# Heads of output groups 0 and 1 back to back, one root for all second-half statistics, and a new order of all queues, in a fused attention and gated-MLP kernel

## The chip, the cores and the metric

The kernel runs on one NeuronCore of one Trainium2 chip. The metric is the device time of one execution in microseconds (us), lower is better.

The engines in the profile: PE is the tensor engine's matmuls, PEld its weight loads, DVE the vector engine, ACT the scalar engine, POOL the GpSimd engine, SP the engine that issues most DMAs. A "q" behind a name means that engine's instruction sequencer.

## The reference

```python
x = A_x                                     # (1, 2048, 512), bf16
xn = layernorm(x)
# A: 32 heads of width 16; each position attends to 8 positions, 2 apart, itself included
q, k, v = split(xn @ wqkv)
attn = softmax(q.k[pos - 2*w] / 4, over w = 0..7)
A = concat(sum_w attn * v[pos - 2*w]) @ wo
# B: a gated MLP whose gate mixes over positions
z  = gelu(xn @ w_in)                        # 2048 x 1376
z1 = z[:, :688];  z2 = layernorm(z[:, 688:])
B = (z1 * (w_sp @ z2 + b_sp)) @ w_out       # w_sp is 2048 x 2048
out = x + A + B
```

## The kernel before

The kernel is written as small steps, each of which emits the instructions of one piece of work, and as one long string, `ORDER`, that lists the steps. Each engine gets its instructions in the order of that string, and in the traces each engine's work stands in that order, so the string is the plan of five queues at once. The 2048 positions are 16 tiles of 128 rows; four tiles form an output group.

The steps that matter here:

| step | engine | what it does |
|---|---|---|
| `z`, `X` | PE | one tile of `xn @ w_in` (second half, first half), 8 matmuls of 344 columns |
| `zg`, `zs` | ACT | gelu of a `z` tile with its sum; its squares with their sum |
| `nw`, `st` | DVE (`st.3`, `st.4`: ACT) | mean, variance and inverse root of the 16 tiles' statistics |
| `N` | DVE | normalise one tile of z2 |
| `p`, `a`, `b` | DVE | products q*k and their sums over the head width |
| `L`, `Lc` | PE, ACT | logits: matmuls in 32-column tiles, then a copy out |
| `V`, `Vc` | PE, ACT | values: matmuls in 32-column tiles, then a copy out |
| `G`, `Gi`, `U`, `T` | PE, ACT, DVE, DMA | gate: 32 matmuls of one tile; plus bias; times z1; transposed by DMA |
| `A` | DVE | 60 products and sums of attention with v, 15 for each group |
| `O`, `Or`, `Oh` | PE | output of a group: heads (64 matmuls in 32-row tiles), remainder (8 matmuls, 24 rows), two halves of 10 full matmuls |
| `Fe`, `F`, `s` | ACT, DVE, DMA | copy a group's output out of PSUM, add x, store |

The program divides eight banks of PSUM, the memory that the matmuls write to: three buffers of two banks (the large pool) and two of one (the small pool).

```python
ps_mm  = ctx.enter_context(tc.tile_pool(name="ps_mm",  bufs=3, space=PSUM))   # 2 banks each
ps_aux = ctx.enter_context(tc.tile_pool(name="ps_aux", bufs=2, space=PSUM))   # 1 bank each
```

The statistics of z2: the twelve tiles of blocks 0 to 2 got their root on the vector engine by Newton's method, the last four on the scalar engine by logarithm and exponential.

```python
def z2_newton(j0, j1):
    b = slice(4 * j0, 4 * j1 + 4)
    y, h, a = zrstd[:, b], zvar[:, b], zm2[:, b]
    turn = [lambda: V.tensor_tensor(a, y, y, ALU.mult),
            lambda: V.scalar_tensor_tensor(a, a, -0.5, h, ALU.mult, ALU.mult),
            lambda: V.scalar_tensor_tensor(y, a, 1.5, y, ALU.add, ALU.mult)]
    return [lambda: V.tensor_scalar(h, h, EPS, None, ALU.add),
            lambda: V.tensor_scalar(y.bitcast(I32), h.bitcast(I32), -0.5, float(0x5f3759df), ALU.mult, ALU.add),
            *turn, *turn, *turn]

def z2_log():                                  # z2_exp follows: exp(-0.5 * log)
    b = slice(12, 16)
    need_table("exp")                          # loads another ACT table where needed
    A.activation(zm2[:, b], zvar[:, b], ACT.Ln, bias=eps_t[:])
```

The heads of a group take two buffers of the large pool; the last group takes one of the large pool, both of the small one, and a cut more.

```python
def out_heads(o):
    last = o == 3
    pos = []
    for tb in range(TB):                                   # TB = 4
        if last and tb >= 2:
            pa = ps_aux.tile([P, TBS], F32, name="pa", tag="aux")
            pos.append(pa[:])
            if tb == 3:
                pb = ps_mm.tile([P, 2, TBS], F32, name="pb", tag="mm")
            continue
        if tb % 2 == 0:
            pmm = ps_mm.tile([P, 2, TBS], F32, name="po", tag="mm")
        pos.append(pmm[:, tb % 2, :])
    # ... (cuts of the last group left out)
    for d in (*range(8, DH), *range(8)):
        for tb in range(TB):
            for pc, cs in cuts[tb]:
                PE.matmul(pc, op[32 * tb:32 * tb + 32, d, o * P:(o + 1) * P],
                          wo_r[32 * tb:32 * tb + 32, d, cs],
                          start=(d == 8), stop=False, tile_position=(32 * tb, 0))
```

Parts of `ORDER`: the logits 5, 6 and 7, the heads of groups 0 and 1, and the end (each ... is a cut):

```
... S0.4 U1 L5 L6 R0 X6 Lc5 ...
... A2 wo1.3 T2 A3 L7 Gi5 ...
... w14 A17 X11 Gi7 T6 A18 O0 Xg11 A19 w10 A20 A21 Or0 Oh0.0 U7 A22 A23 X15 Fe0.0 Fe0.1 F0.0 Oh0.1 A24 s0.0 ...
... A32 s0.1 w15 A33 A34 s0.3 w12 A35 O1 Gi14 A36 T9 U11 A37 xr1 U10 Or1 A38 X14 T8 A39 Oh1.0 ...
... O3 Fe2.2 Fe2.3 F2.2 F2.3 F2.0 s2.3 s2.2 s2.1 s2.0 Or3 Oh3.0 Oh3.1 F3.0 F3.1 s3.0 s3.1 end
```

`end` adds and stores the last three pieces (two from SP, one from ACT).

## Time and profile before

Three runs of the kernel before had a median of 202.78 us (202.71 to 203.77). The span in the table runs from the first to the last instruction of the profiled execution and is about 1.7 us shorter than that execution's time (201.6 against 203.31 us).

| of the profile before | |
|---|---|
| span | 201.6 us |
| PE busy | 197.2 us, 98% |
| DVE busy | 185.4 us, 92% |
| ACT busy | 106.9 us, 53% |
| first z tile starts | 22.66 us |
| last matmul starts | 198.54 us |
| ACT table loads | 10 |

The page's engine line (busy us, share of the span, instructions), and its first line of the chain that ended last:

```profile
PE 197.2 (98%) x1667; PEld 124.9 (62%) x1667; DVE 185.4 (92%) x261; ACT 106.9 (53%) x174; POOL 4.1 (2%) x14
...
PE 93%; DMA 2%; DVE 2%; issue 0%; ACTq 0%
```

A high PE share alone proves little. The Trainium skill ("Perfetto Trace Analysis", "Tensor Engine Instruction (MATMUL, LD_WEIGHTS)") says that a matmul's end in a trace is estimated, not observed, and the same page ("Identifying the Most-Contended Engine") advises against matmul busy time as a measure. The trace agrees: a matmul of 344 columns is recorded as 0.31 us long, and the next one starts after 0.146 us. So I read starts. The next fence is the timeline of PE before, four cuts of it; the columns are start, duration, engine, line, operation, what it writes and reads, shape, and how many instructions were merged:

```profile
108.55 0.40 PE L365 MATMUL pl<-r_pr,rsel 128*32 128x512 bf16 x4
108.88 2.51 PE L240 MATMUL pz<-w_z,xnT 128*128 128x344 bf16 x16
111.23 9.50 PE L454 MATMUL pg<-z,r_qk 128*128 128x344 bf16 x64
120.56 1.33 PE L240 MATMUL pz<-w_z,xnT 128*128 128x344 bf16 x8
121.73 9.50 PE L454 MATMUL pg<-z,r_qk 128*128 128x344 bf16 x64
131.06 1.33 PE L240 MATMUL pz<-w_z,xnT 128*128 128x344 bf16 x8
132.32 3.63 PE L507 MATMUL po<-r_lg,r_pr 32*128 32x512 bf16 x64
135.79 0.60 PE L516 MATMUL po<-r_w,r_uz 24*128 24x512 bf16 x8
136.32 2.33 PE L537 MATMUL po<-r_w,r_uz 128*128 128x512 bf16 x10
...
155.91 3.63 PE L507 MATMUL po<-r_lg,r_pr 32*128 32x512 bf16 x64
...
190.25 0.39 PE L507 MATMUL po<-r_lg,r_pr 32*128 32x512 bf16 x2
...
198.15 0.64 PE L537 MATMUL pb<-r_w,r_uz 128*128 128x224 bf16 x5
```

Compare starts. Eight matmuls of 344 columns take 1.17 us (120.56 to 121.73), but 1.26 us when heads follow (131.06 to 132.32). The 0.09 us more is the way into 32-row mode. The four logits at 108.55 take 0.33 us (0.332 in the single records) where a group of four takes 0.216: the 0.12 us more is the way out. There is no other gap: PE is full from 8.7 us to the end, save for these small steps. I call one way in and out an excursion. Before has eight.

The single records of the weight loads show one thing that differs at such a step. Inside a mode the load for the next matmul starts beside the matmul before it, 144 ns ahead of its own matmul. Before the first heads matmul at 132.32 and before the first full one behind them (136.32) it starts only 4 ns ahead, and so (2 to 5 ns) at every other change of mode in the traces of before.

The vector engine is nearly as full. It waits at 102 us for a gate tile (the bracket gives the idle time before, and what ended it):

```profile
101.93 0.49 DVE L468 TENSOR_TENSOR r_uz<-gs,r_uz 128x640 bf16<-128x640 bf16 x1 [1.62 <-ACT gs L460]
...
186.81 2.55 DVE L433 TENSOR_TENSOR r_pr<-r_pr 128x2048 bf16<-128x2048 bf16 x2
```

The second of these lines ends with the last heads sum, at 189.36 us (186.81 + 2.55). The heads of group 3, which need it, start at 190.25 (in the fence of PE). The slack is 0.9 us.

### The profile page before, as it was taken

The numbers are of one execution on the slowest core, as the hardware profiler recorded it, in microseconds if no ns is written. First come the engines' busy times: TensorE is split into PE (matmuls) and PEld (weight loads), VectorE is DVE, ScalarE is ACT, GpSimd is POOL, SyncE is SP. The second block draws the span as 40 slices with busy tenths as digits, with TensorE's granted clock in tenths as the row PEclk, the third lists the DMA queues.
The fourth block names the chain that finished last, engine by engine and source line by source line (L and its number), as shares of the span: only waits on it lengthen the run. The fifth ranks groups of instructions, "written<-read, shape, count | busy, mean of one in ns | idle before, by whom it ended". The sixth has DMA issues, their size and how long they took to land.

```text
span 201.6 us, 4043 instructions
## 1 busy us (share of the span) xinstructions
PE 197.2 (98%) x1667; PEld 124.9 (62%) x1667; DVE 185.4 (92%) x261; ACT 106.9 (53%) x174; POOL 4.1 (2%) x14
## 2 busy tenths in 40 slices
PE   7899999999999999999999999999999999999994
PEld 2689856656656666666656666644666446664562
DVE  5799699999999999999979999999999999999815
ACT  3575999989999886080383285134712152121400
POOL 3000000400000000000000000000000000000000
PEclk9999999999999999999999999999999999999999
DMA  4994447000794000659949808991243998059363
GB/s 129 340 298 77 90 94 249 0 0 0 134 209 79 0 3 0 125 176 222 205 101 263 166 3 202 195 204 25 75 106 78 234 182 119 0 144 194 77 207 133
DMA packets 66306, 25.91 MB, mean 129 GB/s; under 512 B 56240, under 2 KB 66032, under 8 KB 66032
## 3 DMA queue, kind: packets, MB, share of 16 engines
q1 hardware_dynamic: 65568, 25.19, 55.3%
q10 hardware_dynamic: 720, 0.47, 0.7%
q8 instruction: 13, 0.21, 0.5%
q14 instruction: 5, 0.04, 0.1%
HBM read 10.13 MB, written 2.10 MB: 61 GB/s over the span
## 4 chain that ended last, share of the span: by engine, by line
PE 93%; DMA 2%; DVE 2%; issue 0%; ACTq 0%
PE pg L454 37%; PE pz L240 19%; PE pq L311 13%; PE po L537 8%; PE pv L415 7%; PE po L507 6%; DMA r_x<-in_A_x_dram 2%; PE pl L365 1%; DVE r_pr L525 1%; PE po L516 1%; PE pb L507 1%; DVE stats L211 1%; PE pt L226 1%; ACTq L168 0%; PE pa L311 0%
## 5 line engine op out<-in xcount | busy, mean ns | idle before, releaser
L454 PE MATMUL pg<-z,r_qk 128*128 128x344 bf16 x448 | 66.6, 309 | 0.0
L454 PEld LDWEIGHTS <-r_qk 128*128 128x128 bf16 x448 | 43.8, 98 | 21.8
L240 PE MATMUL pz<-w_z,xnT 128*128 128x344 bf16 x256 | 40.0, 309 | 0.0
L460 ACT ACTIVATE gs<-pg,b_col 128x688 bf16<-128x688 f32 x16 | 13.2, 834 | 48.2 <-PE pg L454 48.2
L429 DVE TENSOR_TENSOR r_pr<-r_x,r_w 128x2048 bf16<-128x2048 bf16 x32 | 38.4, 1219 | 0.3
L433 DVE TENSOR_TENSOR r_pr<-r_pr 128x2048 bf16<-128x2048 bf16 x28 | 34.0, 1218 | 0.4
L240 PEld LDWEIGHTS <-xnT 128*128 128x128 bf16 x256 | 24.6, 98 | 14.4 <-issue 1.9
L311 PE MATMUL pq<-xnT,r_w 128*128 128x256 bf16 (+1 forms) x176 | 29.1, 317 | 0.1
L345 DVE TENSOR_TENSOR r_pr<-r_qk 128x2048 bf16<-128x2048 bf16 x24 | 28.2, 1218 | 0.3 <-ACT r_qk L321 0.3
L311 PEld LDWEIGHTS <-r_w 128*128 128x128 bf16 x184 | 20.2, 114 | 7.4 <-DMA r_w<-in_A_wqkv_dram 0.6
L321 ACT CAST r_qk<-pq 128x1024 bf16<-128x1024 f32 (+1 forms) x16 | 15.4, 990 | 1.9 <-PE pq L311 1.9
L537 PE MATMUL po<-r_w,r_uz 128*128 128x512 bf16 x70 | 16.0, 379 | 0.0
L302 ACT ACTIVATE r_uz<-pz 128x688 bf16<-128x688 f32 x16 | 11.7, 742 | 7.3 <-PE pz L240 7.2
L507 PE MATMUL po<-r_lg,r_pr 32*128 32x512 bf16 x224 | 14.5, 375 | 0.0
L520 ACT CAST r_qk<-po 128x512 bf16<-128x512 f32 x12 | 6.4, 589 | 14.7 <-PE po L537 14.6
L415 PE MATMUL pv<-xnT,r_w 128*32 128x512 bf16 x256 | 14.2, 379 | 0.0
L537 PEld LDWEIGHTS <-r_uz 128*128 128x128 bf16 x85 | 8.1, 98 | 9.3 <-issue 1.1
L354 DVE TENSOR_TENSOR r_pr<-r_pr 128x4096 bf16<-128x4096 bf16 x6 | 13.6, 2286 | 0.0
L211 DVE BATCH_NORM_STATS2 stats<-r_x 128x6 f32<-128x512 bf16 (+1 forms) x18 | 10.9, 615 | 2.0 <-DMA r_x<-in_A_x_dram 2.0
L264 ACT ACTIVATE junk<-z 128x688 bf16<-128x688 bf16 x16 | 12.4, 776 | 0.1
L415 PEld LDWEIGHTS <-r_w 128*32 128x32 bf16 x256 | 9.5, 139 | 4.4
L258 ACT ACTIVATE z<-pz 128x688 bf16<-128x688 f32 x16 | 11.8, 738 | 0.8 <-PE pz L240 0.7
(82 smaller groups left out, 175.5 us busy)
## 6 DMA issues: line engine op xcount, KB each, us to landing
r_lg<-in_A_wo_dram SPq DMA_DIRECT2D x8, 256.0 KB, 4.8
out_dram<-r_qk SPq DMA_DIRECT2D x12, 128.0 KB, 2.7
w_z<-in_B_w_in_dram SPq DMA_DIRECT2D x2, 688.0 KB, 5.4
r_w<-in_A_wqkv_dram SPq DMA_DIRECT2D x2, 512.0 KB, 5.2
r_x<-in_A_x_dram SPq DMA_DIRECT2D x2, 512.0 KB
r_qk<-in_A_x_dram SPq DMA_DIRECT2D x8, 128.0 KB, 2.4
r_w<-in_B_w_out_dram SPq DMA_DIRECT2D x1, 640.0 KB, 5.6
r_w<-in_A_wqkv_dram SPq DMA_DIRECT2D x2, 256.0 KB, 5.3
```

The lines of the kernel that those rows point to most:

```text
L240: PE.matmul(pz[:, hh, 0:FHALF], xnT[:, kc, i * P:(i + 1) * P], wz[:, kc, hh * FHALF:(hh + 1) * FHALF], start=(kc == 0), stop=(kc == C - 1))
L311: PE.matmul(pq[:, cc, p0 * P:(p0 + b1 - b0) * P], wqk[:, sd, kc, c0 + cc:D:C], xv[:, kc, b0:b1, j, :], start=(kc == 0), stop=(kc == C - 1))
L321: cast = A.copy(dst, pq[:, :, p0 * P:(p0 + b1 - b0) * P].rearrange("p c (b t) -> p c b t", b=b1 - b0))
L345: prod = V.tensor_tensor(pr[g % 3][:, c].rearrange("p w b t -> p b w t"), q3.unsqueeze(2).broadcast_to([P, TB, 4, P]), k4, ALU.mult)
L354: V.tensor_tensor(pr[g % 3][:, 0:2], pr[g % 3][:, 0:2], pr[g % 3][:, 2:4], ALU.add)
L415: PE.matmul(pv[32 * tb:32 * tb + 32, dd, :], wv[:, kc, 2 * d2 + dd, :], xnT[:, kc, tb * TBS:(tb + 1) * TBS], start=(kc == 0), stop=(kc == ...
L429: V.tensor_tensor(pw_t[n], vp[:, :, off:off + P], a_sb[:, slot_w(w), ts].unsqueeze(1).broadcast_to([P, DH, P]), ALU.mult)
L433: V.tensor_tensor(pw_t[n] if dst is None else dst, pw_t[n], pw_t[m], ALU.add)
L454: PE.matmul(pg[:, hh, 0:FHALF], wsp[n][:, k, :], z2[:, k, hh * FHALF:(hh + 1) * FHALF], start=(k == 0), stop=(k == NT - 1))
L460: A.activation(gs[:], tiles.pop(("g", n))[:, :, 0:FHALF], ACT.Identity, bias=b_col[:, i:i + 1])
L507: PE.matmul(pc, op[32 * tb:32 * tb + 32, d, o * P:(o + 1) * P], wo_r[32 * tb:32 * tb + 32, d, cs], start=(d == 8), stop=False, tile_positi ...
L537: PE.matmul(pc, uT[:, o % 2, m, tb * P:(tb + 1) * P], wout[:, m, cs], start=False, stop=(m == MCH - 3))
```

## The change

Intent: put the heads of groups 0 and 1 back to back, so that the array changes mode once for both; take one root for all sixteen z2 statistics instead of two; plan all queues anew around that. The heads of group 0 hold two large PSUM buffers, so group 1 must do with one large buffer and both small ones.

```diff
-    nw = z2_var(0, 2) + z2_newton(0, 2)
-    st = z2_var(3, 3) + [z2_log, z2_exp]
+    st = z2_var() + [z2_log, z2_exp]
# z2_newton is gone; z2_var, z2_log and z2_exp lose their slices and take all 16 columns

     def out_heads(o):
         ...
-            if last and tb >= 2:
+            if o in (1, 3) and tb >= 2:
                 pa = ps_aux.tile([P, TBS], F32, name="pa", tag="aux")
                 pos.append(pa[:])
-                if tb == 3:
+                if last and tb == 3:
                     pb = ps_mm.tile([P, 2, TBS], F32, name="pb", tag="mm")
```

and `ORDER`, wholly rewritten; its parts that answer to those shown above:

```diff
+ ... V7 N0.0 Vc3 M0.0 N1.2 M0.1 L5 N0.2 L4 Vc7 ...
+ ... a6 w9 G1 Gi3 Gi4 S0.1 b6 a7 G2 Gi1 w7 U1 S0.2 b7 S0.3 w5 S0.4 Lc5 R0 L6 L7 G6 Lc6 A0 ...
+ ... X12 R1 Xg15 X11 A27 Xg12 w11 A28 O0 Xg11 A29 A30 A31 Or0 O1 A32 A33 A34 Or1 U8 Oh0.0 A35 A36 Oh0.1 Fe0.0 ...
+ ... O3 Fe2.2 Fe2.3 F2.2 F2.1 s2.2 F2.3 s2.1 s2.3 Or3 Oh3.0 Oh3.1 F3.0 F3.1 s3.0 s3.1 s2.0 end
```

Logits 7 now sit next to 6, and 5 next to 4 and the values (`V7`). At the end, store `s2.0` has moved behind `s3.1`.

More of the change, by code (lines that the diff above doesn't have):

```diff
@@ L9 @@
 F32 = mybir.dt.float32
-I32 = mybir.dt.int32
 ACT = mybir.ActivationFunctionType
@@ L42 @@
 ORDER = """
-z1.3 z0.3 p1.2 z1.2 zg1.3 p1.1 zs1.3 q2.1 zg0.3 p0.2 zg1.2 q2.2 p1.3 qc2.1 p0.1 zs0.3 z2.2 qc2.2 p1.0 z0.2
-zg2.2 p0.3 zs1.2 z1.0 zg0.2 p0.0 q2.3 zs2.2 a0 zg1.0 z3.0 qc2.3 z2.1 a1 zg3.0 zs3.0 z0.1 halo zg2.1 b0 z3.3
-zs1.0 b1 q2.0 zg3.3 zg0.1 p2.2 zs0.2 L0 L1 p2.3 X2 qc2.0 p3.2 q3.2 Xg2 zs0.1 p2.0 z2.0 qc3.2 p2.1 z0.0 zg2.0
-p3.3 zs2.1 X1 p3.1 zs2.0 q3.0 zg0.0 p3.0 Xg1 a2 w1 z1.1 qc3.0 zs0.0 z2.3 w0 p4.0 zg1.1 z3.1 zg2.3 b2 zs1.1
-z3.2 w2 nw.0 zg3.1 a3 q3.3 zg3.2 Lc0 w3 zs2.3 nw.1 q3.1 p4.1 qc3.3 nw.2 nw.3 b3 Lc1 X5 qc3.1 X4 zs3.3 p4.3
@@ L48 @@
-zs3.1 L3 nw.4 L2 nw.5 Xg5 V4 nw.6 st.0 p4.2 Lc3 Xg4 nw.7 a4 V5 Vc4 zs3.2 V7 nw.8 p5.2 Vc5 Lc2 nw.9 b4 V0 Vc7
-st.1 nw.10 M0.0 nw.11 st.2 V3 nw.12 p6.3 Vc0 nw.13 N2.2 V2 M0.1 N0.1 st.3 N0.2 st.4 Vc3 N0.3 N0.0 V6 N3.0 Vc2
-N2.3 N1.1 N2.1 L4 N1.0 V1 p5.3 Vc6 Lc4 p5.1 X3 Vc1 N1.3 N3.3 X0 N3.2 N1.2 N2.0 G0.0 N3.1 Xg3 p6.2 Xg0 G0.1
-p5.0 G0.2 p7.2 w4 G2 M0.2 p6.0 late p6.1 M0.3 p7.3 G0.3 Gi2 p7.1 G3 Gi0 p7.0 a5 w8 E0 w5 a6 G4 w9 S0.0 b5 w6
-U0 S0.1 U2 G1 Gi4 S0.2 wo1.0 b6 Gi3 S0.3 a7 X7 Gi1 S0.4 U1 L5 L6 R0 X6 Lc5 T0 b7 G5 xr0 A0 Xg6 A1 T1 Lc6 Xg7
@@ L53 @@
-A2 wo1.3 T2 A3 L7 Gi5 X9 wo1.1 A4 Lc7 w7 X8 mask A5 G6 Xg8 wo1.2 A6 Xg9 A7 A8 M1.0 U5 G8 U4 M1.1 Gi6 M1.2 M1.3
-A9 A10 E1 X10 U3 A11 G9 Gi8 wo0.0 wo0.2 S1.0 wo0.3 wo0.1 U6 T3 Xg10 S1.1 A12 A13 G7 Gi9 A14 w11 A15 S1.2 A16
-w14 A17 X11 Gi7 T6 A18 O0 Xg11 A19 w10 A20 A21 Or0 Oh0.0 U7 A22 A23 X15 Fe0.0 Fe0.1 F0.0 Oh0.1 A24 s0.0 T7 A25
-S1.3 S1.4 G11 A26 Fe0.2 Fe0.3 A27 F0.2 Xg15 U8 s0.2 F0.3 T4 R1 T5 G10 U9 Gi11 A28 A29 A30 A31 G14 Gi10 F0.1
-A32 s0.1 w15 A33 A34 s0.3 w12 A35 O1 Gi14 A36 T9 U11 A37 xr1 U10 Or1 A38 X14 T8 A39 Oh1.0 Xg14 w13 U14 A40
@@ L58 @@
-Oh1.1 Fe1.0 A41 T10 Fe1.1 A42 G12 Fe1.2 F1.1 Fe1.3 A43 A44 A45 F1.2 A46 G15 Gi12 A47 A48 F1.0 A49 G13 F1.3
-Gi15 A50 s1.3 T11 A51 T14 U15 A52 s1.0 xr2 A53 X13 Gi13 A54 X12 s1.1 Xg13 s1.2 A55 T15 O2 Xg12 A56 A57 U13 A58
-Or2 T13 Oh2.0 A59 U12 Oh2.1 T12 Fe2.0 Fe2.1 F2.1 xr3 O3 Fe2.2 Fe2.3 F2.2 F2.3 F2.0 s2.3 s2.2 s2.1 s2.0 Or3
-Oh3.0 Oh3.1 F3.0 F3.1 s3.0 s3.1 end
+z2.0 z1.3 p1.1 z2.2 zg2.0 p0.1 zg1.3 q2.2 zg2.2 p0.3 zs2.2 q2.3 p1.2 qc2.2 p1.3 q2.1 qc2.3 p1.0 z1.0 p0.2
+qc2.1 w3 z2.1 p0.0 zg1.0 zs1.0 q2.0 p2.2 zg2.1 a1 z2.3 qc2.0 w2 z1.2 zg2.3 p2.3 halo zs2.0 z3.0 p2.0 zg1.2
@@ new lines @@
+z1.1 w0 zg3.0 b1 z0.1 zg1.1 p2.1 zs2.3 X0 a0 zg0.1 z3.2 Xg0 zs1.1 z3.3 a2 zg3.2 z3.1 zs1.2 zg3.3 z0.2 b0 zg3.1
+X4 b2 zg0.2 zs3.3 L0 L1 Xg4 q3.1 p3.2 zs3.1 p3.0 Lc0 q3.0 Lc1 p3.1 qc3.1 q3.2 p3.3 qc3.0 zs0.1 a3 z0.3 qc3.2
+q3.3 zg0.3 p4.1 zs1.3 p4.0 z0.0 qc3.3 X1 p4.2 zg0.0 zs0.3 X2 p4.3 Xg1 X5 st.0 zs2.1 st.1 a4 Xg2 L2 V6 zs0.2
+zs3.2 b3 Xg5 V2 b4 Vc6 zs0.0 p5.3 L3 V5 zs3.0 p5.2 Vc2 V1 st.2 p5.1 Vc5 p5.0 V0 st.3 a5 w4 Lc2 Vc1 V4 st.4 Vc0
+w1 N1.1 V3 N2.0 Vc4 N1.0 b5 Lc3 V7 N0.0 Vc3 M0.0 N1.2 M0.1 L5 N0.2 L4 Vc7 N3.3 X6 N0.1 M0.2 N0.3 late X3 N3.1
@@ new lines @@
+N1.3 N2.1 G0.0 N2.2 Xg6 N2.3 N3.2 N3.0 G0.1 p7.1 G0.2 M0.3 G0.3 p7.2 G4 p6.0 Gi0 w6 Lc4 p6.3 Xg3 p6.2 E0 p7.3
+G3 p6.1 U0 S0.0 p7.0 a6 w9 G1 Gi3 Gi4 S0.1 b6 a7 G2 Gi1 w7 U1 S0.2 b7 S0.3 w5 S0.4 Lc5 R0 L6 L7 G6 Lc6 A0 Gi2
+Lc7 U2 U4 mask T4 U3 M1.0 A1 T2 G7 A2 Gi6 w8 A3 wo1.2 A4 T0 A5 X7 M1.1 Gi7 A6 wo1.3 xr0 G5 A7 Xg7 A8 w10 M1.2
+A9 w12 U7 A10 X8 Gi5 A11 X10 T1 A12 G8 Xg10 A13 Xg8 wo1.0 A14 T7 M1.3 A15 G9 Gi8 A16 A17 E1 A18 A19 wo0.2
+wo0.3 G10 wo0.1 U6 wo1.1 U5 Gi9 wo0.0 A20 T3 S1.0 S1.1 A21 X9 S1.2 G12 A22 S1.3 Gi10 T5 A23 S1.4 T6 A24 Xg9
@@ new lines @@
+w15 A25 X15 A26 Gi12 w14 X12 R1 Xg15 X11 A27 Xg12 w11 A28 O0 Xg11 A29 A30 A31 Or0 O1 A32 A33 A34 Or1 U8 Oh0.0
+A35 A36 Oh0.1 Fe0.0 A37 Fe0.1 A38 G14 Fe0.2 Fe0.3 F0.2 F0.0 F0.1 s0.0 A39 s0.1 F0.3 A40 xr1 A41 Oh1.0 w13 A42
+U10 Oh1.1 Fe1.0 U9 T8 Gi14 A43 Fe1.1 A44 T10 X13 A45 G11 s0.2 T9 A46 s0.3 F1.0 A47 A48 G13 F1.1 Gi11 s1.1 Xg13
+U11 U12 Fe1.2 A49 T12 A50 A51 X14 A52 G15 Xg14 Fe1.3 U14 Gi13 F1.3 F1.2 A53 s1.2 T11 A54 T14 A55 O2 Gi15 s1.0
+A56 U15 U13 T15 A57 Or2 xr2 Oh2.0 A58 A59 s1.3 Oh2.1 T13 Fe2.0 Fe2.1 xr3 F2.0 O3 Fe2.2 Fe2.3 F2.2 F2.1 s2.2
@@ L62 @@
+F2.3 s2.1 s2.3 Or3 Oh3.0 Oh3.1 F3.0 F3.1 s3.0 s3.1 s2.0 end
 """
@@ L264, in z2_sq, with z2_var @@
         A.activation(junk[:], z2[:, i, :], ACT.Square, accum_out=zsq[:, q:q + 1])
-    def z2_var(j0, j1):
-        b = slice(4 * j0, 4 * j1 + 4)
-        return [lambda: V.tensor_scalar(zmean[:, b], zsum[:, b], 1.0 / FH, None, ALU.mult),
-                lambda: V.tensor_tensor(zm2[:, b], zmean[:, b], zmean[:, b], ALU.mult),
-                lambda: V.scalar_tensor_tensor(zvar[:, b], zsq[:, b], 1.0 / FH, zm2[:, b], ALU.mult, ALU.subtract)]
-    def z2_newton(j0, j1):
-        b = slice(4 * j0, 4 * j1 + 4)
-        y, h, a = zrstd[:, b], zvar[:, b], zm2[:, b]
-        turn = [lambda: V.tensor_tensor(a, y, y, ALU.mult),
-                lambda: V.scalar_tensor_tensor(a, a, -0.5, h, ALU.mult, ALU.mult),
-                lambda: V.scalar_tensor_tensor(y, a, 1.5, y, ALU.add, ALU.mult)]
-        return [lambda: V.tensor_scalar(h, h, EPS, None, ALU.add),
-                lambda: V.tensor_scalar(y.bitcast(I32), h.bitcast(I32), -0.5, float(0x5f3759df), ALU.mult, ALU.add),
-                *turn, *turn, *turn]
+    def z2_var():
+        return [lambda: V.tensor_scalar(zmean[:], zsum[:], 1.0 / FH, None, ALU.mult),
+                lambda: V.tensor_tensor(zm2[:], zmean[:], zmean[:], ALU.mult),
+                lambda: V.scalar_tensor_tensor(zvar[:], zsq[:], 1.0 / FH, zm2[:], ALU.mult, ALU.subtract)]
     def z2_log():
-        b = slice(12, 16)
         need_table("exp")
-        A.activation(zm2[:, b], zvar[:, b], ACT.Ln, bias=eps_t[:])
+        A.activation(zm2[:], zvar[:], ACT.Ln, bias=eps_t[:])
     def z2_exp():
-        b = slice(12, 16)
         need_table("exp")
-        A.activation(zrstd[:, b], zm2[:, b], ACT.Exp, scale=-0.5)
+        A.activation(zrstd[:], zm2[:], ACT.Exp, scale=-0.5)
     def z2_norm(j, tb):
@@ L661 @@
     ap = [f for o in range(4) for f in apply_ops(o)]
-    nw = z2_var(0, 2) + z2_newton(0, 2)
-    st = z2_var(3, 3) + [z2_log, z2_exp]
+    st = z2_var() + [z2_log, z2_exp]
     steps = {"z": z2_mm, "zg": z2_gelu, "zs": z2_sq, "q": qk_mm, "qc": qk_cast, "p": prod_c, "a": pair_add, "b": pair_add2,
              "L": logits, "Lc": logits_cast, "V": v_mm, "Vc": v_cast, "X": z1_mm, "Xg": z1_gelu,
-             "nw": lambda k: nw[k](), "st": lambda k: st[k](), "N": z2_norm,
+             "st": lambda k: st[k](), "N": z2_norm,
              "M": sm_max, "E": sm_exp, "S": lambda h, k: sm_sum(h, k), "R": sm_norm, "mask": add_mask,
```

## The prediction

> **What bounds the kernel now.** The tensor engine, with almost nothing left to fill. The page gives PE busy 98% of the span; the chain of waits is PE work in program order from 9.06 to 196.7 us (PE 93%). In the PE timeline I find no wait over about 0.1 us after 8.7 us: a gate tile of 32 matmuls always takes 4.67 us, a z tile 1.17, a heads stretch 3.45. Ahead of it x is loaded, behind it come the last adds and stores (5 us); the change leaves both alone but for one store. The vector engine is second: in its timeline no gap is over 1.7 us from 24.6 to 189 us, and its last heads sum ends at 189.3 us, 1 us ahead of heads 3 (190.25).
>
> **What the PE still loses.** Entry to and exit from each stretch of 32-column or 32-row matmuls. A z tile takes 1.17 us, but 1.26 when heads follow (131.06 to 132.32): 0.09 us. The eight remainder matmuls take 0.53 us (135.79 to 136.32) where two groups of 0.216 would take 0.43: 0.10. Logits 7 alone take 0.33 us (108.55 to 108.88) for one group: 0.11. So an excursion costs about 0.20 us. This agrees with the Trainium skill, "TensorEngine Tiling (Array Packing)", Key Properties: changing the tiling mode drains the engine (no figure given). Before has eight: logits 0-1; logits 2-4 with the values; logits 5-6; logits 7; four heads stretches.
>
> **What the change does.**
> - Heads 0 and 1 become one stretch; logits 5 join the values, 7 joins 6. Six excursions: 2 x 0.20 = 0.4 us off the PE, all on the critical path. No matmul is added or removed.
> - The Newton root goes: 14 vector instructions of 0.165 us, some 1.7 us back to back. Gain on the path none; slack before heads 3 grows from 1 to 2 us or more.
> - The scalar engine changes to its exp table and back three times instead of four: 2 x 1.28 us less, off the path (53% busy).
> - Heads 0 and 1 hold all eight PSUM banks. The next gate tile needs two evacuations of 0.5 us; they run under the 2.16 us of group 0's second full half: fits with 0.9 us.
> - One root waits for the last square. Adding durations: normalised blocks 0 to 3 at about 77, 78, 79.5, 80.5 us, wanted at 78.9, 80.1, 81.2, 82.4: slack 1 to 2 us.
> - Heads 1 start at 147.6 us instead of 155.9; their sums should be done near 146. Slack 1.5 us; the gelu of tile 12 ahead of heads 0 has about 0.3.
> - Store 2.0 now issues among the last ones: 0 to 0.2 us at the end.
>
> **Predicted time.** 202.78 - 0.4 plus a little for small new waits: 202.4 us. 8 times in 10 between 201.9 and 203.2. Faster by over 2%: 1%; within 2%: 97%; slower by over 2%: 2%.
>
> **What would show it.** Right: six tiled stretches with 0.2 us of overhead each; heads 3 near 189.8 us; no PE wait over 0.1 us; vector busy about 183 us; eight table loads. Wrong: PE waits before heads 1 on the vector engine, before the first gate tile on a normalisation, before the gate tile after heads 1 on an evacuation; a later last store.
>
> **What would make it wrong.** Any slack smaller than my sums, since PE has no spare time to regain a wait; weight-block transposes landing late in the new order of the one issuing queue; run-to-run spread (202.71 to 203.77) over a gain of 0.2%.

## The result, and the profile after

The changed kernel ran at a median of 203.32 us (202.72 to 203.58, six runs) against 202.93 (202.71 to 203.77, six runs) before. The ratio is 1.0012 with a 95% interval of 0.9989 to 1.0035: the same. The median lies 0.1 us above the range that I gave; the ratio times the 202.78 us that I started from gives 203.0, inside it.

The traces are far more exact than the times. I cut each span into three: up to the first z tile (the "head", whose program is the same in every kernel here), from the first z tile's start to the last matmul's start (the "PE stretch"), and from there to the end (the "tail"). The last matmul is the fifth of the last merged line of PE (198.15 before, 197.81 after), so these numbers come from the trace's single records:

| us | head | PE stretch | tail | span without head |
|---|---|---|---|---|
| before | 22.66 | 175.88 | 3.06 | 178.94 |
| after | 22.74 | 175.46 | 3.36 | 178.82 |
| difference | +0.08 | -0.42 | +0.30 | -0.12 |

The PE stretch gained just what was expected. Most of it is gone again by the end.

The page after, engine line and chain:

```profile
PE 196.2 (97%) x1667; PEld 124.7 (62%) x1667; DVE 184.4 (91%) x247; ACT 103.7 (51%) x172; POOL 18.3 (9%) x14
...
PE 92%; DMA 4%; DVE 1%; issue 0%; SPq 0%
```

POOL's rise from 4.1 to 18.3 us is one instruction, the cast of the gate's bias (2.06 us before, 16.24 after). It ends at 53 us and the bias is first read at 84, so it holds nothing up; why it takes longer I did not trace.

The timeline of PE after, around the joined heads:

```profile
102.38 0.61 PE L350 MATMUL pl<-r_pr,rsel 128*32 128x512 bf16 x8
...
140.27 3.66 PE L238 MATMUL pz<-w_z,xnT 128*128 128x344 bf16 x24
143.87 3.63 PE L492 MATMUL po<-r_lg,r_pr 32*128 32x512 bf16 x64
147.33 0.60 PE L501 MATMUL po<-r_w,r_uz 24*128 24x512 bf16 x8
147.76 0.38 PE L492 MATMUL po<-r_lg,r_pr 32*128 32x512 bf16 x2
147.77 0.38 PE L492 MATMUL pa<-r_lg,r_pr 32*128 32x512 bf16 x2
...
151.75 4.49 PE L522 MATMUL po<-r_w,r_uz 128*128 128x512 bf16 x20
156.08 4.83 PE L439 MATMUL pg<-z,r_qk 128*128 128x344 bf16 x32
...
189.91 0.39 PE L492 MATMUL po<-r_lg,r_pr 32*128 32x512 bf16 x2
...
197.81 0.64 PE L522 MATMUL pb<-r_w,r_uz 128*128 128x224 bf16 x5
```

The remainder of group 0 takes 0.43 us (147.33 to 147.76): two groups of four, no way out, because group 1 (half in `po`, half in `pa`, the small pool) follows in the same mode. At 102.38 logits 6 and 7 stand together. There are six excursions. No PE wait over 0.1 us appears after the head.

The vector engine after, the lines that answer to the two of before:

```profile
102.83 1.23 DVE L414 TENSOR_TENSOR r_pr<-r_x,r_w 128x2048 bf16<-128x2048 bf16 x1 [0.95 <-PE pl L350]
...
143.17 3.68 DVE L418 TENSOR_TENSOR r_pr<-r_pr 128x2048 bf16<-128x2048 bf16 x3
...
185.13 3.68 DVE L418 TENSOR_TENSOR r_pr<-r_pr 128x2048 bf16<-128x2048 bf16 x3
```

It still waits at 102 us, now for logits on PE (for a gate tile from ACT before). Group 1's last sum ends at 146.85 us, 0.9 us ahead of its heads (147.76). The last heads sum of all ends at 188.81, 1.1 us ahead of heads 3 (189.91).

The tail, as the timeline of SP's queue shows it, before:

```profile
197.38 2.20 SPq L532 DMA_DIRECT2D out_dram<-r_pr  x4
```

and after:

```profile
197.04 0.93 SPq L517 DMA_DIRECT2D out_dram<-r_pr  x2
198.03 0.42 SPq L517 DMA_DIRECT2D out_dram<-r_qk  x1
198.54 0.89 SPq L517 DMA_DIRECT2D out_dram<-r_pr  x2
```

The middle line, `out_dram<-r_qk`, is store 2.0. It stands between the stores of group 3.

### The profile page after: what moved, and what is told of

Its sections match the earlier page's. It is cut to its first block, busy times and chain, and to the rows that moved or that the text cites. A ratio compares the mean times of both kernels' runs of the same rounds, so it can differ in the third digit from the quotient of the medians. Undisturbed runs are those within 1.5% of the kernel's fastest.

```text
span 201.6 us, 4025 instructions
## 1 busy us (share of the span) xinstructions
PE 196.2 (97%) x1667; PEld 124.7 (62%) x1667; DVE 184.4 (91%) x247; ACT 103.7 (51%) x172; POOL 18.3 (9%) x14
## 4 chain that ended last, share of the span: by engine, by line
PE 92%; DMA 4%; DVE 1%; issue 0%; SPq 0%
PE pg L439 37%; PE pz L238 19%; PE pq L296 13%; PE pv L400 7%; PE po L522 7%; PE po L492 6%; DMA r_w<-in_A_wqkv_dram 3%; DMA r_x<-in_A_x_dram 1%; PE pa L522 1%; PE pl L350 1%; DVE r_pr L510 1%; PE po L501 1%; PE pb L492 1%; PE pa L296 0%; PE pt L224 0%
## 5 line engine op out<-in xcount | busy, mean ns | idle before, releaser
L238 PE MATMUL pz<-w_z,xnT 128*128 128x344 bf16 x256 | 39.3, 309 | 0.0
L631 POOL CAST b_col<-b 128x16 f32<-128x16 bf16 x1 | 16.2, 16244 | 34.1 <-DMA b<-in_B_b_sp_dram 34.1
L505 ACT CAST r_qk<-po 128x512 bf16<-128x512 f32 x10 | 5.5, 587 | 22.7 <-PE po L522 22.7
L522 PE MATMUL po<-r_w,r_uz 128*128 128x512 bf16 x60 | 13.6, 380 | 0.0
```

The lines of the kernel that those rows point to most:

```text
L238: PE.matmul(pz[:, hh, 0:FHALF], xnT[:, kc, i * P:(i + 1) * P], wz[:, kc, hh * FHALF:(hh + 1) * FHALF], start=(kc == 0), stop=(kc == C - 1))
L522: PE.matmul(pc, uT[:, o % 2, m, tb * P:(tb + 1) * P], wout[:, m, cs], start=False, stop=(m == MCH - 3))
L631: G.tensor_copy(b_col[:], b16[:])
```

## The experiments

Two theories for the lost gain, before any run. A: store 2.0, at its new place, holds the issuing queue while the last stores wait, and so gives back 0.3 us. B: the tail differed by chance. Beside them stood the question whether an excursion really costs 0.2 us, and what the vector engine's saved work is worth.

All traces, in one table; "ratio" is to the kernel before of the same rounds:

| run | head | PE stretch | tail | span without head | ratio (95% interval) |
|---|---|---|---|---|---|
| before | 22.66 | 175.88 | 3.06 | 178.94 | |
| changed | 22.74 | 175.46 | 3.36 | 178.82 | 1.0012 (0.9989 to 1.0035) |
| a0_changed_again | 22.98 | 175.46 | 3.35 | 178.81 | 0.9990 (0.9964 to 1.0016) |
| e1_store_early | 22.88 | 175.46 | 3.07 | 178.53 | 0.998 (0.9953 to 1.0007) |
| e2_before_store_late | 23.52 | 175.88 | 3.34 | 179.22 | 1.0007 (0.9979 to 1.0036) |
| e3_heads_apart | 22.04 | 175.67 | 3.07 | 178.75 | 1.001 (0.9988 to 1.0031) |
| e4_five_more | 23.14 | 176.61 | 3.05 | 179.67 | 1.005 (1.0027 to 1.0074) |
| e5_before_heads_joined | 23.12 | 177.33 | 3.05 | 180.38 | 1.0071 (1.0044 to 1.0098), wrong result |
| e5b_heads_joined_mended | 22.22 | 177.52 | 3.07 | 180.59 | 1.0093 (1.0028 to 1.0159) |
| e6_dve_early | 22.93 | 175.46 | 3.07 | 178.53 | one run |
| e7_dve_late | 23.39 | 177.18 | 3.06 | 180.25 | 1.0091 (1.0067 to 1.0114) |
| e8_more_tables | 23.58 | 175.46 | 3.07 | 178.53 | one run |

Where a part of a kernel is the same, its column repeats to 0.02 us. The head does not: it runs from 22.04 to 23.58 us, with the same program in every row.

### a0: the changed kernel once more

> The changed kernel as it is, once more, as the measure for the runs beside it. From the two traces: first z tile to last matmul 175.46 us against 175.88 before (-0.42), last matmul to end of span 3.36 us against 3.06 (+0.30). If both repeat, ratio to before about 0.9995; if the tail was chance, the tail is 3.1 and the ratio 0.998.

Measured: 203.14 us (median of six), ratio 0.9990. PE stretch 175.46 and tail 3.35, both as in the first trace. The tail is not chance.

### e1: store 2.0 early

```diff
- ... s2.2 F2.3 s2.1 s2.3 Or3 Oh3.0 Oh3.1 F3.0 F3.1 s3.0 s3.1 s2.0 end
+ ... s2.2 F2.3 s2.1 s2.3 s2.0 Or3 Oh3.0 Oh3.1 F3.0 F3.1 s3.0 s3.1 end
```

> The changed kernel with store 2.0 put back among the other stores of group 2, ahead of the last matmuls. Theory A (that store, issued between the last group's stores, holds the issuing queue and gives back the gain): last matmul to end 3.06 us as before, z-to-last-matmul still 175.46, ratio to before 0.998. Theory B (the tail differed by chance or by how data lands): tail stays near 3.36 and the ratio equals that of the changed kernel, about 1.000.

Measured: 202.92 us (202.66 to 203.67), ratio 0.998. The tail is back at 3.07, PE stretch 175.46, span without head 178.53, which is 0.41 us under before. It is the store's place that costs, as theory A says; how, e2 shows. SP's queue in e1:

```profile
197.19 2.20 SPq L517 DMA_DIRECT2D out_dram<-r_pr  x4
```

The four stores take 2.20 us from the first issue to the end of the last, as before the change.

### e2: the kernel before, store 2.0 late

```diff
- ... F2.0 s2.3 s2.2 s2.1 s2.0 Or3 Oh3.0 Oh3.1 F3.0 F3.1 s3.0 s3.1 end
+ ... F2.0 s2.3 s2.2 s2.1 Or3 Oh3.0 Oh3.1 F3.0 F3.1 s3.0 s3.1 s2.0 end
```

> The kernel before with only store 2.0 moved to the place that it has in the change (after 3.0 and 3.1, before the last three). Theory A: tail grows from 3.06 to about 3.35 us, z-to-last-matmul 175.88 unchanged, ratio 1.0015. Theory B: tail unchanged, ratio 1.000.

Measured: 203.46 us, ratio 1.0007 (interval wide enough for both theories). The trace decides: tail 3.34, PE stretch 175.88. One store at that place costs 0.28 us in the old plan and 0.29 in the new one.

Two parts can be told apart in the traces of before, the changed kernel (twice), e1 and e2. From the last matmul's start to the last store's issue it is 0.72 us with store 2.0 early, 0.84 with it late: 0.12 to 0.13 us in the queue. From that issue to the last DMA packet's end it is 1.17 us early, 1.30 to 1.31 late: 0.13 to 0.14 us in issuing it and in the transfers. The last 0.02 to 0.05 us come behind the last packet. The Trainium skill names a cause for each half. "Trainium Kernel Development and Optimization", Key Constraints: the queues all run on the same 16 DMA engines and interleave. "Perfetto Trace Analysis", DMA Instruction (HWDGE): the reported time of an issue includes the wait for the lock of the descriptor generator. The traces agree. A store of group 3 from SP takes 0.33 us to issue when alone, and 0.40 us after the change, where the pushed-back one (198.54) meets the one that ACT issues (198.61). The last store's issue, too, takes 0.39 to 0.40 us instead of 0.33, so some 0.06 us of the second part is still issuing.

The packets show the transfers, counted here from the last matmul's start. Store 2.0's packets run from 0.8 to 1.3 us after the change, where e1 has those of group 3's third store. That store's packets run from 1.3 to 1.7 instead, and those of ACT's store from 1.51 to 1.97 instead of 1.30 to 1.67, though ACT issues it at 0.41 in both. How much of this is a wait for the engines, and how much for the descriptor generator, is not told apart.

### e3: heads apart again

```diff
- ... A29 A30 A31 Or0 O1 A32 A33 A34 Or1 U8 Oh0.0 A35 A36 Oh0.1 Fe0.0 ...
+ ... A29 A30 A31 Or0 A32 A33 A34 U8 Oh0.0 A35 A36 Oh0.1 O1 Or1 Fe0.0 ...
```

(on top of e1)

> The changed kernel with store 2.0 early and the heads of groups 0 and 1 apart again (group 0's full matmuls between). Theory A: seven excursions, z-to-last-matmul 175.46 + 0.20 = 175.66, no new wait. Rival (joining is worth nothing, the saving is from the logits or the rest of the plan): 175.46 as with the heads joined.

Measured: PE stretch 175.67, 0.21 us more than e1, seven excursions, no new wait. Joining the heads alone is worth 0.21 us; the other half of the 0.42 us is then the joined logits (by subtraction: no run took the logits apart again). Two excursions account for the whole gain, so by this sum nothing of it is left for the saved vector work or the saved table loads. The ratio, 1.001 (0.9988 to 1.0031), could not have shown this.

### e4: five excursions more

```diff
-    def out_heads(o):
+    def out_heads(o, part=None):          # the heads loop in parts: d = 8..11, 12..15, 0..7
- ... L0 L1 Xg4 q3.1 ... X5 ... L2 V6 ... V2 ... Or0 O1 ... Or1 U8 Oh0.0 ... G15 ... O2 Gi15 ...
+ ... L0 Xg4 q3.1 L1 ... L2 V6 X5 ... V2 ... Or0 Oh0.0 O1 ... Or1 U8 ... G15.0 G15.1 ... O2.0 G15.2 O2.1 G15.3 O2.2 Gi15 ...
```

(on top of e1)

> The changed kernel with store 2.0 early and five more excursions: a z tile between value tiles, a q tile between logits 0 and 1, group 0's first full half between heads 0 and 1, heads 2 in three pieces between quarters of the last gate tile. Same matmuls. Theory A: eleven excursions, each 0.2 us on PE: z-to-last-matmul 175.46 + 1.0 = 176.46, ratio to before about 1.003. Rival (the entry and exit gaps overlap other work): within 0.2 us of 175.46.

Measured: 204.22 us, ratio 1.005 (1.0027 to 1.0074). Eleven excursions, PE stretch 176.61: 1.15 us more than e1, 0.23 us for each of the five. The suspected cost is real, it adds up, and here it is also clear of the noise of the times. It came out 0.15 us above my 1.0. By start-to-start times three of the five cost 0.22 us each, the one at the value tiles 0.26 (a value tile was delayed by 0.05 us on top) and the one at the q tile 0.24. So an excursion is 0.21 to 0.22 us rather than 0.20: the first full matmul behind it takes 0.01 us more.

### e5 and e5b: the heads joined in the old plan

Group 0's heads, evacuations, adds and stores were moved down to group 1's place, with half of group 1 in the small pool; nothing else of the change.

```diff
- ... X11 Gi7 T6 A18 O0 Xg11 A19 w10 A20 A21 Or0 Oh0.0 U7 ...      (and Fe0, F0, s0 behind it)
- ... w12 A35 O1 Gi14 A36 T9 U11 A37 xr1 U10 Or1 A38 X14 ...
+ ... w12 A35 O0 Or0 O1 Gi14 A36 T9 U11 A37 U10 Or1 Oh0.0 A38 Oh0.1 Fe0.0 Fe0.1 A39 Fe0.2 Fe0.3
+     F0.0 F0.1 F0.2 F0.3 xr1 s0.0 s0.1 s0.2 s0.3 X14 ...
```

> The kernel before, its own plan, with only the heads of group 0 moved down to those of group 1 and half of group 1 in the small pool. Theory A (an excursion costs about 0.2 us of PE, and the plan has slack for it): seven excursions, z-to-last-matmul 175.88 - 0.20 = 175.68, tail 3.06, ratio 0.999. Rival (the join needs the whole new plan): new PE waits of 0.5 us or more ahead of heads 0, heads 1 or the tiles behind them, z-to-last-matmul above 176, ratio above 1.001.

Measured: a wrong result (relative error 0.20) and a PE stretch of 177.33 us. The wrong result was my mistake: the transposed gate product has two buffers, one for each parity of the group, and I left the transpose of tile 9 (group 2) ahead of group 0's last read. The program is race-free then, it just overwrites. The time shows a PE wait of 1.5 us for the gelu of tile 15, which itself waited 7.0 us for the transpose of the buffer that it overwrites: its matmuls had moved too far forward.

The mended try puts that transpose behind the read, tile 15 behind gate tile 14, and the products of tiles 8 and 9 a little earlier.

> The kernel before, heads of groups 0 and 1 joined alone, mended: the transpose of tile 9 after group 0's last read of the same buffer (the wrong result of the first try), tile 15's matmuls and gelu after gate tile 14 (its 1.7 us PE wait), the products of tiles 8 and 9 a little earlier. Theory A (the join is worth one excursion in either plan): seven excursions, z-to-last-matmul 175.88 - 0.21 = 175.67, tail 3.06. Rival (the join needs the whole new plan): a PE wait of over 0.2 us is left, z-to-last-matmul 175.9 or more.

Measured: correct, 204.68 us, ratio 1.0093 (1.0028 to 1.0159). Seven excursions, and no wait around the joined heads. But PE stretch 177.52, 1.64 us more than before. The three waits that tell why, from the lists of waits of PE, DVE and ACT in e5b (who waited <- for whom, us in total, times, longest):

```profile
PE po L506 <- DVE r_pr L432: 1.8, 1, 1.8
```

```profile
DVE r_qk L526 <- ACT r_qk L519: 2.3, 1, 2.3
```

```profile
ACT r_qk L519 <- DMA out_dram<-r_qk: 6.3, 2, 4.6
```

Read upwards. ACT may not copy group 1's output into the four row buffers until group 0's stores have left them. DVE, in order, waits for ACT with the add. The last heads sum is late by that, and heads 3 wait 1.8 us. So 0.2 us were won and 1.8 lost. The rival was right here: in this plan the join alone does not pay. That it would pay with the adds and stores spread anew, as the change has them, was not tried in the old plan.

### e6 and e7: more vector work, early and late

```diff
- ... p6.1 U0 S0.0 p7.0 ...                e6: one sum of the first softmax twice
+ ... p6.1 U0 S0.0 S0.0 p7.0 ...
- ... A20 T3 S1.0 S1.1 A21 ...             e7: one sum of the second softmax three times
+ ... A20 T3 S1.0 S1.0 S1.0 S1.1 A21 ...
```

(each on top of e1; repeating the sum gives the same result)

> The changed kernel, store 2.0 early, with 1.14 us more vector work (one pair sum of the first softmax repeated) ahead of 102 us. Resynchronisation theory (the vector engine meets a wait for PE at about 102 us, so work saved ahead of it buys nothing later): the wait before the first heads product, 0.95 us, vanishes; last heads sum ends about 0.2 us later (189.0), PE unchanged. Additive theory (vector work saved anywhere widens the slack before heads 3): last sum ends 1.1 us later, 189.95, and heads 3 begin about 0.1 us later.

> The changed kernel, store 2.0 early, with 2.27 us more vector work (one pair sum of the second softmax done three times) after 102 us. Both theories: nothing absorbs it; the slack of 1.1 us before heads 3 is used up, last heads sum ends about 191.1, heads 3 begin about 1.2 us later, z-to-last-matmul about 176.6, ratio to before about 1.004. If another wait of the vector engine after 102 us absorbs it, PE is unchanged.

e6 measured: PE stretch 175.46, and the last heads sum ends 166.08 us after the first z tile, the same as in e1. The added sum took 1.23 us (I had counted 1.14), and nothing of it arrives there. The list of waits of DVE in e1 has this line, and in e6 it is gone:

```profile
DVE r_pr L414 <- PE pl L350: 1.0, 1, 1.0
```

So the vector engine meets PE at 102 us and waits for it; work saved or added ahead of that changes the length of this wait and, as far as the wait is long enough, nothing behind it. (I expected 0.2 us to pass. Compared instruction by instruction with e1, the added sum delays the engine by 1.27 us; a wait for a gate tile at 99 us takes up 0.23 of that, the wait for the logits 0.85, and the last 0.19 go at the next gate tile, 1.4 us behind the logits.)

e7 measured: 205.07 us, ratio 1.0091. Last heads sum 2.5 us later (168.60 us after the first z tile), PE stretch 177.18, 1.72 us more. The list of waits of PE in e7:

```profile
PE pz L238 <- ACT r_uz L287: 0.7, 1, 0.7
PE po L492 <- DVE r_pr L418: 0.6, 1, 0.6
```

Late vector work is paid for, more than I expected (1.2), and at another place: by start-to-start times PE loses 0.86 us in the z tiles ahead of heads 0 (their gelu stands behind the softmax on ACT) and 0.81 us between heads 0 and heads 1 (group 1's sums). The slack that runs out first is the one ahead of the joined heads.

### e8: two more table changes

```diff
- ... G8 Xg10 ...  s1.1 Xg13 ...
+ ... G8 tab Xg10 ...  s1.1 tab Xg13 ...        # tab: need_table("exp"); the gelu loads its own again
```

(on top of e1)

> The changed kernel, store 2.0 early, with two more changes of the scalar engine's table to exp and back (four loads, 5.1 us of scalar time), ahead of the gelu of tiles 10 and 13. Theory A (the table loads that the change saved lie off the path): z-to-last-matmul stays 175.46. Rival (they hold PSUM banks and so the PE): it grows by 0.3 us or more.

Measured in one look: twelve table loads against eight, PE stretch 175.46. At these two places four more loads cost nothing. That the two which the change saved, at another place, bought nothing was not run; it is argued from the sum in e3, where two excursions account for the whole gain. (This run's device time, 203.82 us, is high, but so is its head, 23.58 us; without the head it is e1's 178.53.)

### Where the spread of the times comes from

No run was made for this; it is read from the traces that were. The longest heads come with this wait in the timeline of PE (here e8):

```profile
8.70 0.60 PE L296 MATMUL pq<-xnT,r_w 128*128 128x256 bf16 x4
10.89 0.52 PE L296 MATMUL pq<-xnT,r_w 128*128 128x256 bf16 x3 [1.60 <-DMA r_w<-in_A_wqkv_dram]
```

and in e3, which has the shortest head, the same place has none:

```profile
8.55 0.39 PE L224 MATMUL pt<-ident,r_x 128*128 128x128 bf16 x4
8.78 2.41 PE L296 MATMUL pq<-xnT,r_w 128*128 128x256 bf16 x19
```

PE waited for this weight transfer 1.6 us at a head of 23.58, 1.4 at 23.52 and 23.39, 1.1 at 23.14, 0.7 at 22.74, 0.2 at 22.22 and not at all at 22.04; the four others (22.88 to 23.12) waited 0.7 to 1.2. Before's own trace (22.66) has none of it either, but other small waits for x, and such waits of up to 0.6 us stand in other traces too, so the head doesn't follow this wait alone. The transfer landed at 10.85 us in e8 and at 9.31 in e3. The time at which the weights of k land in the first 11 us varies from execution to execution by 1.5 us, more than three times the gain of this change. Why it varies stays open. This is shown for the twelve profiled executions only.

## Why the prediction was right or wrong

- **Same within 2%: right,** and for the stated reason: PE had almost nothing left to fill. It was also an easy call, since 2% is 4 us and the sum of all stated terms is a tenth of that.
- **"Six excursions: 2 x 0.20 = 0.4 us off the PE": right.** PE stretch -0.42 us, repeated in four traces; +0.21 by undoing the heads (e3); +1.15 for five more (e4). Heads 3, expected near 189.8 us, start at 189.91.
- **"Store 2.0 now issues among the last ones: 0 to 0.2 us at the end": the term that was mis-sized.** It measured 0.28 us (e2) to 0.29 us (changed against e1). The range has room for the time in the issuing queue (0.12 to 0.13 us), but not for what comes on top: the stores behind it issue more slowly and their packets land later (0.13 to 0.14 us), because store 2.0's 128 KB move ahead of them. With 0.42 won and 0.30 given back, 0.12 us is left, which no set of runs here could show as a time.
- **"slack before heads 3 grows from 1 to 2 us or more": wrong.** It went from 0.9 to 1.1 us. I had let 1.7 us of saved vector work run through to the end. Both plans have a wait at about 102 us (for a gate tile that ACT hands on from PE before, for logits from PE after), and work ahead of it does not reach the end (shown in the new plan, by e6). It did no harm, because the slack was not needed.
- **"Slack 1.5 us" before heads 1: too large,** 0.9 us. With e7 this is one of the two places that run out first.
- **Gelu of tile 12, 0.3 us ahead of heads 0; two evacuations with 0.9 us in hand; z2 normalised at 80.5 us: right.** In the trace: 143.54 against 143.87 us; the second evacuation ends at 155.19 against the gate tile's start at 156.08; the last normalisation ends at 80.57.
- **Eight table loads instead of ten, off the path: right** (e8, for loads at other places). **Vector engine busy about 183 us: too low,** 184.4, which is 1.0 us less than before.
- **The absolute time** of 202.4 us rested on a median of three runs that was at the low end: all six had 202.93, later sets 203.39, 203.16 and 202.84.

The version that keeps the gain is e1, the changed kernel with store 2.0 early: 0.41 us shorter than before and 0.29 shorter than the change, by the spans without head. Its ratio, 0.998 (0.9953 to 1.0007), has not cleared the noise. That it is faster is shown by the traces, not by the times.

Not run: the joined heads without the small pool's half. By the program's text group 1 would then need a buffer that group 0 frees only after matmuls that stand behind group 1 in PE's own queue, so I expect that program never to end.

## What to carry to other kernels

When one engine is full from end to end, count what its starts cost beyond the work itself; a change of the array's mode, there and back, at 0.2 us is such a cost, and sorting the order so that like stands with like takes it off. Then follow the gain to the last store: a piece of work that "only fills a gap" among the last stores can be on the critical path twice, in the issuing queue and in the transfers. And when an engine waits for another somewhere in the middle, work saved ahead of that wait is not slack behind it.

## What the Trainium skill lacked or had wrong

- "TensorEngine Tiling (Array Packing)", Key Properties, says that changing the tiling mode drains the engine, without a figure: here 0.21 to 0.22 us for one way in and out, about half at each end (0.09 in, 0.10 to 0.12 out, 0.01 on the first matmul behind).
- "TensorE: Matmul & The Clock Gate", Back-to-back issue gap, gives about 131 ns for a matmul of 512 columns in a real stream of weight load and matmul. Here such pairs start 216 ns apart (344 columns: 146 ns), which is that page's formula for the isolated gap, 2.5 ns plus one column per 1/2.4 ns.
- The same page, Part 3, has a measured speedup of 3.07 for four row tiles of 512 columns. Here 64 matmuls of 32 rows take 3.46 us, 216 ns for each four, the time in which one full matmul of 512 columns follows another: a factor of four in a steady stream.
- None of the pages that I read gives the price of a store that is issued among the last ones: 0.28 to 0.29 us for 128 KB here, 0.12 to 0.13 of it in the queue and 0.13 to 0.14 in the issue and the transfers behind it.
